# A retention and gated-MLP kernel on one core: a new instruction list for its first three blocks, chunk sums moved into another batch's results, words instead of drains, and a last tile in two halves

## The chip, the core and the metric

The kernel runs on one core of a Trainium2 chip. The metric is the device time of one execution in microseconds; before the change the median of three runs was 320.49 us (320.16 to 321.43). The engines are named here as the profile names them: PE is TensorE (PEld its weight loads), DVE is VectorE, ACT is ScalarE, POOL is GpSimd, SP is SyncE, whose queue issues most transfers.

## What is computed

For 8 batches, 8 heads, 576 positions and head size 64, a retention layer, and then a two-layer network over all 4608 rows of 512 columns:

```python
scores = scale * np.matmul(q, k.transpose(0, 1, 3, 2))
Dmat = np.where(rel >= 0, gamma[:, None, None] ** rel[None, :, :], 0.0)
attn = np.matmul(scores * Dmat[None, :, :, :], v)
x = attn.transpose(0, 2, 1, 3).reshape(B * S, H * D)
h = x @ w_in
s = np.sin(alpha * h)
g = h + s * s / (alpha + 1e-09)
out = g @ w_out
```

The decay `gamma ** rel` factors into powers of the row's and of the column's position, so that inside a chunk of 128 positions only a 0/1 mask is left, and earlier chunks enter by a state of 64 by 64 numbers for each head.

## The kernel before

The output has nine blocks of 512 rows. Blocks 0 to 7 are the first 512 positions of batches 0 to 7; block 8 gathers the last 64 positions of all eight batches ("the ends"). A block has 16 units. In a unit u TensorE projects 128 of the 2048 hidden columns (`project`, four matmuls of 128x512, line 486), ScalarE takes the sine (line 494), the square is made on VectorE, ScalarE or GpSimd (lines 503 and 505), and VectorE forms `ss/alpha + h`, the "product" (line 510). The second product, `gemm2` (line 530), adds four matmuls of 128x512 a unit; four of its units finish a tile of 128 rows, which `finish` copies (line 102) and stores. In the loop the second product of block n-1 runs in the units of block n.

The attention of batch n+1 is done during block n. k, q and v are loaded as float32 (line 113), scaled and cast (line 161, v line 104), and k and q are transposed: by TensorE for batches 0 and 1 (`turn`, line 194, and `take`), by a transposing transfer for the others (`crossed`, line 184). `scores` (line 318) makes a quarter of a batch's scores, `masked` (line 329) multiplies the mask. `outer` (line 266) makes the four chunk sums, `evict` copies them to SBUF, and `chain` turns them on GpSimd into states (`more`, `to_state`, lines 293 to 301). `values` (line 356) multiplies the masked scores with v, in a first call for the rows of one half of TensorE (`same` false) and a second for the other half (`same` true); both halves write the same PSUM bank, and so the second call waits with `nc.tensor.drain()` until the first is out of TensorE. `add_states` (line 374) adds the states' part, `keep` copies the result to the input of `project`.

PSUM has eight banks: two double banks "mm" for scores, sums and results, three banks "hp" for projections, one bank "op" for the second product. Under one tag the banks are handed out in turn.

Every engine runs its queue in the order in which the program names its steps. For the start and blocks 0 to 2 (from line 561 on) this order is a list written out step by step; from block 3 on it is a loop over units with steps attached (`at_unit`: after the sine of unit u; `behind`: at the end of unit u). Loads, stores and transposing transfers go out on SyncE's queue, the weights on GpSimd's (`load_w_in`, `load_w_out`, four groups each). The raw float32 buffers are six, so a load waits for an earlier cast. `wait_for_w_out(0)`, a small transfer that reads w_out's first group, stands on SyncE's queue between batch 0's loads and batch 1's. In the loop before, units 0, 4, 8 and 12 hold attention: scores; sums and scores; scores and the first values; the other values and the states.

## Time and profile before

| | |
|---|---|
| median of three runs | 320.49 us |
| the profiled execution | 320.69 us |
| its span, first to last instruction | 318.9 us |
| TensorE busy | 301.3 us (94%) |
| VectorE busy | 216.9 us (68%) |
| ScalarE busy | 174.0 us (55%) |
| GpSimd busy | 137.3 us (43%) |
| moved by DMA | 49.96 MB |

The profile is of one execution. Rows of the timeline give the start and the length in us, then engine, line, operation, and the tile written and those read; a bracket holds the idle time before it and what ended that. Rows that group instructions give their count, the busy time in us and the mean in ns. Ends of matmuls are modelled, so distances between starts are the safer measure on TensorE.

### The profile page before, as it was taken

Reading aid. Unit: us, or ns where it says so; the run is one execution under the profiler, and the core shown is the slowest. Engines: PE = TensorE matmul, PEld = TensorE weight load, DVE = VectorE, ACT = ScalarE, POOL = GpSimd, SP = SyncE. Lnnn points to the kernel's source line nnn. Section 1 sums busy time; section 2 is a strip of 40 time slices with the busy share of each in tenths; the row PEclk is TensorE's granted clock in tenths of the full one; section 3 lists DMA queues with packets and bytes.
Section 4 is the critical chain, followed back from the end, with each engine's and each line's share of the span. In section 5 each row is a group of like instructions: output and inputs, shape, how many; then the busy total and the mean of one; then the engine's idle time right before and its main releaser. Section 6 shows DMA issues by size and latency. Waiting matters only on the chain.

```text
span 318.9 us, 7711 instructions
## 1 busy us (share of the span) xinstructions
PE 301.3 (94%) x3180; PEld 143.9 (45%) x3180; DVE 216.9 (68%) x316; ACT 174.0 (55%) x269; POOL 137.3 (43%) x140
## 2 busy tenths in 40 slices
PE   7889999699799999999999999999999999999994
PEld 2554454244344444444444444444444444444442
DVE  2778877669468989687878787878746565655500
ACT  3548654498356645464547454745465565456411
POOL 0866542472866961993299329922720000000000
PEclk9999999799999999999999999999999999999999
DMA  8999999999994559996999589952352111111232
GB/s 211 266 202 209 299 242 280 218 239 232 213 248 144 84 113 251 262 171 134 245 255 184 123 240 257 155 113 67 72 82 49 35 35 33 36 33 34 57 77 66
DMA packets 103108, 49.96 MB, mean 157 GB/s; under 512 B 44944, under 2 KB 98592, under 8 KB 103072
## 3 DMA queue, kind: packets, MB, share of 16 engines
q1 hardware_dynamic: 98352, 45.12, 63.1%
q0 software_dynamic: 4224, 4.19, 8.0%
q8 instruction: 25, 0.41, 0.6%
q10 hardware_dynamic: 496, 0.15, 0.2%
q14 instruction: 11, 0.09, 0.1%
HBM read 36.85 MB, written 9.44 MB: 145 GB/s over the span
## 4 chain that ended last, share of the span: by engine, by line
PE 78%; DMA 9%; DVE 6%; ACT 2%; POOL 2%; issue 2%; ACTq 0%; POOLq 0%; DVEq 0%
PE hps L486 35%; PE ops L530 34%; DMA v<-in_v_dram 5%; DMA q<-in_q_dram 3%; PE sc L318 2%; PE o L356 2%; DVE gT L510 2%; DVE ret L329 2%; DVE ss_t L505 1%; DMA k<-in_k_dram 1%; PE kv L266 1%; ACT s_t L494 1%; PE o L374 1%; PE idle L543 1%; ACT ss_t L503 1%
## 5 line engine op out<-in xcount | busy, mean ns | idle before, releaser
L494 ACT ACTIVATE s_t<-hps,alpha_t 128x512 f16<-128x512 f32 x144 | 97.9, 685 | 97.1 <-PE hps L486 96.7
L530 PE MATMUL ops<-w_out,gT 128*128 128x512 f16 x580 | 144.0, 378 | 0.9 <-ACT osb L102 0.5
L510 DVE SCALAR_TENSOR_TENSOR gT<-ss_t,inva,hps 128x512 f16<-128x512 f16 x144 | 106.1, 746 | 49.4 <-ACT ss_t L503 42.1
L486 PE MATMUL hps<-xT,w_in 128*128 128x512 f16 (+1 forms) x520 | 129.3, 380 | 3.6 <-DVE xT L104 2.1
L486 PEld LDWEIGHTS <-w_in 128*128 128x128 f16 x584 | 56.8, 98 | 71.2 <-issue 5.9
L530 PEld LDWEIGHTS <-gT 128*128 128x128 f16 x580 | 54.3, 98 | 64.5 <-DVE gT L510 0.9
L505 DVE TENSOR_TENSOR ss_t<-s_t 128x512 f16<-128x512 f16 x88 | 54.0, 614 | 17.3 <-ACT s_t L494 17.2
L329 DVE TENSOR_TENSOR ret<-sc,mask 128x1024 f16<-128x1024 f32 x32 | 38.6, 1218 | 1.7 <-PE sc L318 1.6
L293 POOL TENSOR_TENSOR s<-kvs,cn 128x256 f16<-128x256 f32 x20 | 13.4, 670 | 49.4 <-ACT kvs L102 47.1
L161 POOL TENSOR_TENSOR k<-k,cn 128x1024 f16<-128x1024 f32 (+1 forms) x13 | 24.8, 1911 | 17.3 <-DMA k<-in_k_dram 17.3
L102 ACT COPY osb<-ops 128x512 f32<-128x512 f32 (+1 forms) x36 | 20.5, 573 | 16.8 <-PE ops L530 14.2
L503 ACT ACTIVATE ss_t<-s_t 128x512 f16<-128x512 f16 x45 | 28.3, 631 | 0.6
L161 POOL TENSOR_TENSOR q<-q,cn 128x1024 f16<-128x1024 f32 (+1 forms) x15 | 27.3, 1822 | 1.1 <-DMA q<-in_q_dram 1.0
L102 ACT CAST xT<-o 128x1024 f16<-128x1024 f32 (+1 forms) x16 | 13.6, 881 | 13.0 <-PE o L374 12.8
L505 POOL TENSOR_TENSOR ss_t<-s_t 128x512 f16<-128x512 f16 x11 | 11.3, 1039 | 13.4 <-ACT s_t L494 12.7
L486 PE MATMUL hps<-xS,w_in 128*128 128x512 f16 x64 | 16.4, 379 | 0.0
L104 POOL CAST v<-v 128x1024 f16<-128x1024 f32 (+1 forms) x12 | 13.0, 1084 | 6.5 <-DMA v<-in_v_dram 6.5
L301 POOL TENSOR_TENSOR kvs<-s,kvs 128x256 f32<-128x256 f32 x19 | 15.1, 792 | 1.5
L356 PE MATMUL o<-ret,v 64*64 64x128 f16 x512 | 13.0, 220 | 1.8 <-issue 0.6
L300 POOL TENSOR_TENSOR s<-kvs,cn 128x256 f32<-128x256 f32 x19 | 12.1, 635 | 2.8 <-ACT kvs L102 2.7
L318 PE MATMUL sc<-qT,kT 64*64 64x128 f16 x512 | 12.1, 220 | 0.7 <-DVE qT L104 0.4
L356 PEld LDWEIGHTS <-v 64*64 64x64 f16 x512 | 8.8, 106 | 7.9 <-issue 7.8
(52 smaller groups left out, 126.7 us busy)
## 6 DMA issues: line engine op xcount, KB each, us to landing
out_dram<-osb SPq DMA_DIRECT2D x70, 128.0 KB, 2.4
k<-in_k_dram SPq DMA_DIRECT2D x16, 512.0 KB, 6.7
q<-in_q_dram SPq DMA_DIRECT2D x16, 512.0 KB, 6.4
v<-in_v_dram SPq DMA_DIRECT2D x16, 512.0 KB, 7.1
w_in<-in_moe_w_in_dram POOLq DMA_DIRECT2D x4, 512.0 KB, 8.1
w_out<-in_moe_w_out_dram POOLq DMA_DIRECT2D x4, 512.0 KB, 10.0
ks<-in_k_dram SPq DMA_DIRECT2D x8, 128.0 KB, 5.8
qs<-in_q_dram SPq DMA_DIRECT2D x8, 128.0 KB, 3.8
```

The lines of the kernel that those rows point to most:

```text
L102: eng.copy(d_, s_)
L161: eng.tensor_tensor(dst[:, a0:a1].rearrange("p a r t d -> p t (a r) d"), t_.rearrange("p (t a) x -> p t a x", t=2)[:, :, a0:a1].rearrange( ...
L301: nc.gpsimd.tensor_tensor(self.kvs[:, c], s32, self.kvs[:, c], ADD)
L318: matmul(sc[halves(g), t, c : c + 128], kT[halves(t), 2 * a + r, halves(g)], qT[halves(t), 2 * a : 2 * a + 2, halves(g)], start=(z == 0 an ...
L329: nc.vector.tensor_tensor(ret.rearrange("p t (z x) -> p (t z) x", z=2), sc.rearrange("p t (z x) -> p (t z) x", z=2), mask[:, 0:256].unsque ...
L356: matmul(o[t][halves(e), c : c + 128], v16[halves(g), 4 * t + 2 * x + e, r, :], self.ret[p, x][halves(g), t, m : m + 128], start=(not same ...
L486: matmul(hps_of[n, fc][0][:, cols], w_in16[:, a, fc * P : (fc + 1) * P], xs[n][:, a, cols], start=(a == 0 and part != 1), stop=(a == KT - ...
L494: nc.scalar.activation(s_t, hps, mybir.ActivationFunctionType.Sin, bias=0.0, scale=alpha_t[:, fc : fc + 1],)
L503: nc.scalar.activation(ss_t, s_t, mybir.ActivationFunctionType.Square)
L505: eng.tensor_tensor(ss_t, s_t, s_t, MULT)
L510: nc.vector.scalar_tensor_tensor(gT[n][:, fc, :], ss_t, inva[:, fc : fc + 1], hps, MULT, ADD)
L530: matmul(ops[n, c][:, cols], gT[n][:, fk, c * P : (c + 1) * P], w_out16[:, fk, cols], start=(fk == 0 and cols.start == 0), stop=(fk == FC ...
```

## The change

Six things are altered together.

1. The list for the start and blocks 0 to 2 is written anew: the order of loads, casts, projections, units of the second product and attention, which engine casts and squares, and how many filling matmuls there are (29 instead of 31). `wait_for_w_out(0)` is gone; a `wait_for_w_out(2)` stands late in block 1. Many projections are made in two halves of 256 columns.
2. Each of the eight PSUM banks has a tag of its own (h0, h1, h2, op, m0, m1), and each step names its bank; the list uses all of them for projections.
3. In the loop, for n from 3 to 5, the chunk sums of batch n+2 are made in unit 12, among the results of batch n+1, into the bank of the second product and one projection bank. Scores go to units 3 and 8 (block 3 keeps 0, 4 and 8). The second product's units 12 and 13 both run behind projection 13. Loads and casts move some units, and squares of units 4, 5, 6, 8 and 9 go to ScalarE in blocks with attention.
4. In the loop the drain between the two calls of `values` is replaced: an empty instruction on GpSimd or SyncE waits for the last matmul of the first call, and the first matmul of the second call waits for it.
5. The ends of batches 0 to 3 and 4 to 7 each get one double bank and are done together, scores in unit 1, values and states in unit 8.
6. The last tile is made as two halves of 256 columns in two banks; the second half's store is issued by ScalarE.

Between the first projection and batch 1's last masked scores VectorE's queue now holds 16 products, 6 squares, 4 masked scores, four half casts of k and q, and five smaller copies and scalings; TensorE's holds 16 projections, 9 units of the second product, 4 sets of eight transposes, 64 score matmuls and 64 of chunk sums. From the second masked score of batch 2 to the end of the list VectorE's holds 7 masked scores, 18 products and 5 squares besides copies and casts, TensorE's 18 projections' worth and 14 units of the second product besides attention.

On SyncE, at the start, behind the first loads of batch 0. The names are tiles of k, q and v of batch 0, then of batch 1; before:

```order
5 L113 DMA v_96<-in_v_dram 128x8x128
6 L113 DMA v_98<-in_v_dram 128x8x128
7 L558 DMA gate<-w_out_72 128x64
8 L113 DMA k_462<-in_k_dram 128x8x128
9 L113 DMA q_464<-in_q_dram 128x8x128
```

and now:

```order
5 L114 DMA v_191<-in_v_dram 128x8x128
6 L114 DMA v_245<-in_v_dram 128x8x128
7 L114 DMA q_378<-in_q_dram 128x8x128
8 L114 DMA k_464<-in_k_dram 128x8x128
9 L114 DMA k_537<-in_k_dram 128x8x128
```

The small transfer that read w_out is gone from between the two batches.

On GpSimd at the same place, casts (q, k, v), states (s, kvs) and the issue of weights; before:

```order
7 L161 TENSOR_TENSOR k_165<-k_92,cn 128x2x4x64
8 L92 DMA w_in_71<-in_moe_w_in_dram 128x4x512
9 L161 TENSOR_TENSOR q_200<-q_94,cn 128x2x8x64
10 L92 DMA w_in_71<-in_moe_w_in_dram 128x4x512 x2
11 L300 TENSOR_TENSOR s_270<-kvs,cn 128x256
12 L301 TENSOR_TENSOR kvs<-s_270,kvs 128x256
13 L293 TENSOR_TENSOR s_273<-kvs,cn 128x256 x2
14 L95 DMA w_out_72<-in_moe_w_out_dram 128x4x512
15 L92 DMA w_in_71<-in_moe_w_in_dram 128x4x512
```

and now:

```order
12 L93 DMA w_in_71<-in_moe_w_in_dram 128x4x512
13 L105 CAST v_247<-v_245 128x1024
14 L316 TENSOR_TENSOR s_303<-kvs,cn 128x256
15 L317 TENSOR_TENSOR kvs<-s_303,kvs 128x256
16 L309 TENSOR_TENSOR s_365<-kvs,cn 128x256
17 L316 TENSOR_TENSOR s_369<-kvs,cn 128x256
18 L317 TENSOR_TENSOR kvs<-s_369,kvs 128x256
19 L309 TENSOR_TENSOR s_365<-kvs,cn 128x256
20 L93 DMA w_in_71<-in_moe_w_in_dram 128x4x512
21 L162 TENSOR_TENSOR k_534<-k_464,cn 128x2x4x64
22 L93 DMA w_in_71<-in_moe_w_in_dram 128x4x512
23 L96 DMA w_out_72<-in_moe_w_out_dram 128x4x512
```

The third group of w_in now stands behind the states of batch 0, and the fourth, with the first of w_out, behind a half cast of batch 1's k.

The list is not shown further; two of its lines stand for it in the diff below.

```diff
-        wait_for_w_out(0)
-        load(1, "k", 0)
+        load_w_in(2)
+        load(1, "q", 0)
...
+    def order(later, earlier):
+        tc.add_manual_dep(
+            later.ins,
+            earlier.ins.name,
+            mybir.DependencyInfo(mybir.DependencyClass.Sync, mybir.DependencyReason.DATA),
+            reason="rows of the two halves take turns at a bank",
+        )
+
+    def told(last, eng):
+        mark = eng.nop()
+        order(mark, last)
+        return mark
...
+        def evict_bank(self, g, eng):
+            copy(
+                eng,
+                self.kvs.rearrange("p (x g) a d -> p g x (a d)", g=2)[:, g],
+                self.banks[g].rearrange("p (x y) -> p x y", x=2),
+            )
...
+            if not same and relay is not None:
+                self.mark[p] = told(made[-1], relay)
+            elif p in self.mark:
+                order(made[0], self.mark[p])
...
+    def finish(n, c, eng=None, cols=slice(0, 512), issue=None):
...
+            (issue or nc.sync).dma_start(rows_of(n, c)[r, :, cols], osb[halves(r), cols])
...
+                if n == 3:
+                    at_unit(0, lambda: A.scores(0, 0, next(m)), lambda: A.scores(0, 1, next(m)))
...
+                    at_unit(4, lambda: A.outer((0, 1), next(m)), lambda: A.scores(1, 0, next(m)), lambda: A.evict((0, 1)))
...
+                else:
+                    at_unit(3, lambda: A.scores(0, 0, next(m)), lambda: A.scores(0, 1, next(m)))
...
+                    at_unit(8, lambda: A.scores(1, 0, next(m)), lambda: A.scores(1, 1, next(m)))
...
+                at_unit(12, lambda: A.values(0, False, next(m), relay=G_), lambda: A.values(1, False, next(m), relay=S_ if n < 6 else G_))
+                if n < 6:
+                    at_unit(12, lambda: at[n + 2].outer((0, 1), "op", next(h)))
+                at_unit(12, lambda: A.values(0, True), lambda: A.add_states(0), lambda: A.values(1, True), lambda: A.add_states(1))
...
+                    at_unit(12, lambda: at[n + 2].evict_bank(0, A_))
+                at_unit(12, lambda: A.keep(0, A_))
...
+                    at_unit(12, lambda: at[n + 2].evict_bank(1, A_))
+                    behind(12, lambda: at[n + 2].chain((0, 1, 2, 3)))
+                behind(13, lambda: A.keep(1, A_))
...
+                if n < 6:
+                    at_unit(3 + i, lambda nm=nm, p=p: cast(n + 2, nm, int(p), G_))
...
+                at_unit(8, lambda: E[0].values(False, next(m)), lambda: E[1].values(False, next(m)))
+                at_unit(8, lambda: E[0].values(True), lambda: E[1].values(True))
+                at_unit(8, E[0].add_states, E[1].add_states)
...
-        for u in range(15):
-            gemm2(NBLK - 1, u, "hp")
-            if u % 4 == 3:
-                finish(NBLK - 1, u // 4)
-        for cols in (slice(0, 256), slice(256, 512)):
-            gemm2(NBLK - 1, 15, "hp", cols)
-            finish(NBLK - 1, 3, cols=cols)
+        for c in range(3):
+            tag = next(h)
+            for u in range(4 * c, 4 * c + 4):
+                gemm2(NBLK - 1, u, tag)
+            finish(NBLK - 1, c)
+        for cols, issue in ((slice(0, 256), nc.sync), (slice(256, 512), nc.scalar)):
+            tag = next(h)
+            for u in range(12, 16):
+                gemm2(NBLK - 1, u, tag, cols)
+            finish(NBLK - 1, 3, cols=cols, issue=issue)
```

More of the change, by code (lines that the diff above doesn't have):

```diff
@@ L1 @@
 from contextlib import ExitStack
+from itertools import cycle
 import numpy as np
@@ L335, in masked, with values @@
             self.ret[p, y] = ret
-        def values(self, p, same, spare=False):
+        def values(self, p, same, *tags, relay=None):
             if same:
@@ L608 @@
[L608 to L622 removed]
+        cast(0, "q", 1, V)
+        load_w_in(0)
+        turn(0, "k", 1, "h1")
@@ new lines @@
+        take(0, "k", 1, A_)
+        at[0].scores(0, 1, "m0")
+        keep_busy(4, "h2")
+        load(0, "v", 0)
+        at[0].masked(0, 1)
+        turn(0, "q", 1, "h2")
+        take(0, "q", 1, V)
+        cast(0, "v", 0, G_)
+        at[0].outer((0,), "op", "h0")
+        load_w_in(1)
+        at[0].take_sum(0, A_)
+        load(0, "v", 1)
+        cast(0, "v", 1, G_)
+        at[0].scores(1, 0, "m1")
+        at[0].outer((1,), "op", "h1")
+        at[0].masked(1, 0)
+        at[0].take_sum(1, A_)
@@ new lines @@
+        product(0, 13)
+        at[1].masked(0, 0)
+        take(1, "q", 1, A_)
+        cast(1, "v", 0, G_)
+        at[1].outer((0,), "m1")
+        at[1].take_sum(0, A_)
+        at[1].take_sum(1, A_)
+        at[1].to_state(0, V)
+        load_w_out(3)
+        gemm2(0, 5, "h0")
+        at[1].scores(0, 1, "m1")
+        at[1].masked(0, 1)
+        at[1].scores(1, 0, "m0")
+        gemm2(0, 13, "op")
+        gemm2(0, 14, "op")
+        gemm2(0, 6, "h0")
+        cast(1, "v", 1, V, (0,))
+        at[1].masked(1, 0)
@@ L839 @@
+        sine(1, 4)
+        project(1, 11, "h1")
+        sine(1, 11)
+        square(1, 4, V)
+        product(1, 4)
+        finish(0, 2, V)
+        project(1, 8, "op", 0)
+        project(1, 8, "op", 1)
+        at[2].scores(0, 0, "m1")
+        at[2].masked(0, 0)
         sine(1, 8)
-        square(1, 8, V)
+        square(1, 8, A_)
+        square(1, 11, A_)
         product(1, 8)
-        cast(3, "k", 1, G_)
-        crossed(3, 0, "q")
-        load(4, "v", 1)
-        load(4, "k", 0)
-        at[2].scores(0, 0)
@@ new lines @@
+        square(2, 2, A_)
+        gemm2(1, 9, "h2")
+        at[3].scores(0, 0, "m1")
+        sine(2, 1)
+        at[3].outer((0, 1), "m0")
+        square(2, 3, V)
+        project(2, 7, "h1")
+        product(2, 3)
+        product(2, 2)
+        sine(2, 5)
+        square(2, 5, G_)
+        square(2, 1, V)
+        product(2, 1)
+        at[3].masked(0, 0)
+        at[3].evict((0, 1), A_)
+        at[3].more(1)
+        at[3].more(2)
+        product(2, 5)
+        cast(4, "q", 0, G_, (1,))
```

924 lines of the change are left out of this document (447 added, 477 removed).

## The prediction

> **What bounds the kernel now.** I read the stages first: a table of windows from the first projection on, cut at the end of block 0's projections, at the late start of block 1's, inside the list and at the start of block 3. Columns are the stretch, its length, the busy time of TensorE, of its weight loads, of VectorE, ScalarE and GpSimd, the granted clock, the DMA share and GB/s.
>
> ```profile
> 19.89:31.30 11.41, 11.41 (x61) 5.97 (x61) 8.75 (x18) 8.85 (x14) 6.10 (x7) 1.00 1.25 208
> 31.30:59.17 27.87, 23.46 (x326) 12.18 (x325) 22.34 (x36) 13.51 (x22) 13.16 (x11) 1.00 1.14 272
> 59.17:88.00 28.83, 25.87 (x303) 11.41 (x303) 19.21 (x27) 19.70 (x32) 16.08 (x16) 0.94 1.01 221
> 88.00:115.52 27.52, 26.89 (x321) 12.42 (x319) 22.30 (x29) 17.33 (x27) 21.66 (x22) 1.00 0.71 149
> 115.52:147.14 31.62, 31.52 (x344) 15.15 (x345) 25.78 (x34) 17.24 (x26) 20.85 (x21) 1.00 0.96 205
> ```
>
> TensorE is the bound. From 115.52 us on (the loop) it idles 0.1 us in a block of 31.6, so there the time is the work itself. The written-out list for blocks 0 to 2 is another matter: TensorE idles 4.41 us between 31.30 and 59.17, 2.96 up to 88.00 and 0.63 up to 115.52, 8.0 us in all. The timeline shows the longest of these waits, and two more windows show what it drags behind it.
>
> ```profile
> 59.17 7.46 PE L486 MATMUL hps<-xT,w_in 128*128 128x512 f16 x26 [2.12 <-DVE xT L104]
> 56.00:60.00 4.00, 1.58 (x6) 0.53 (x5) 2.56 (x2) 0.41 (x2) 3.42 (x3) 0.93 1.16 225
> 60.00:64.00 4.00, 4.00 (x13) 1.52 (x12) 2.78 (x5) 2.63 (x4) 0.00 (x0) 0.64 0.92 210
> ```
>
> After 2.12 us without a matmul the granted clock (third column from the end) is 0.93 in one window and 0.64 in the next: 4 x 0.07 + 4 x 0.36 = 1.7 us of matmul time lost. So 8.0 + 1.7 = 9.7 us is all that a better order of the list can win back after the first projection; the number of projections and of matmuls of the second product in it stays.
>
> The wait stands behind a chain of transfers. The first row below is from the timeline of SyncE: behind batch 0's last load stands a small transfer that waits for w_out, and so the first load of batch 1 goes out at 26.16. The windows show what the two kinds do to each other: weights alone move 207 GB/s, loads alone 289, and with both in flight 190. Then come the queue table for 42 to 46 us (q0 carries weights, q1 the loads) and, from the page, the size of one group of w_in.
>
> ```profile
> 26.16 0.53 SPq L113 DMA_DIRECT2D k<-in_k_dram  x1
> 22.00:26.00 4.00, 4.00 (x21) 1.81 (x19) 2.96 (x6) 3.82 (x7) 1.30 (x2) 1.00 1.24 207
> 36.00:40.00 4.00, 3.29 (x28) 1.84 (x26) 3.96 (x5) 2.04 (x5) 3.74 (x3) 1.00 1.11 289
> 42.00:46.00 4.00, 3.41 (x88) 2.22 (x90) 2.84 (x4) 2.10 (x4) 1.11 (x2) 1.00 1.09 190
> q0 software_dynamic: 493, 0.50, 82.6%
> q1 hardware_dynamic: 519, 0.26, 26.7%
> ```
>
> ```profile
> w_in<-in_moe_w_in_dram POOLq DMA_DIRECT2D x4, 512.0 KB, 8.1
> ```
>
> **The change part by part: the list.** Without the gate, batch 1's first loads go out as soon as batch 0's buffers are cast, some 15 us earlier than 26.16 by my estimate, so its data no longer ends last. What is late next? Between the first projection and batch 1's last masked scores, the new queues hold what the section on the change counts, and these groups, one of VectorE's fullest windows and three rows of TensorE's timeline give the durations.
>
> ```profile
> L510 DVE SCALAR_TENSOR_TENSOR gT<-ss_t,inva,hps 128x512 f16<-128x512 f16 x144 | 106.1, 746 | 49.4 <-ACT ss_t L503 42.1 <-POOL ss_t L505 3.9
> L505 DVE TENSOR_TENSOR ss_t<-s_t 128x512 f16<-128x512 f16 x88 | 54.0, 614 | 17.3 <-ACT s_t L494 17.2
> L329 DVE TENSOR_TENSOR ret<-sc,mask 128x1024 f16<-128x1024 f32 x32 | 38.6, 1218 | 1.7 <-PE sc L318 1.6
> L161 DVE TENSOR_TENSOR k<-k,cn 128x512 f16<-128x512 f32 x2 | 1.7, 851 | 0.3 <-DMA k<-in_k_dram 0.3
> L194 PE MATMUL tr<-ident,k 128*128 128x128 f16 x32 | 2.5, 219 | 1.1 <-DVE gT L510 0.7 <-DVE k L161 0.4
> 70.00:80.00 10.00, 9.26 (x161) 4.27 (x150) 9.19 (x12) 8.75 (x14) 4.30 (x4) 1.00 0.96 247
> 19.89 7.95 PE L486 MATMUL hps<-xT,w_in 128*128 128x256 f16 x44 [0.16 <-ACT xT L102]
> 296.68 1.03 PE L486 MATMUL hps<-xS,w_in 128*128 128x512 f16 x4
> ...
> 298.41 1.03 PE L486 MATMUL hps<-xS,w_in 128*128 128x512 f16 x4
> ```
>
> VectorE: 16 products x 0.746 = 11.9, 6 squares x 0.614 = 3.7, 4 masked x 1.218 = 4.9, 4 half casts of q and k x 0.85 = 3.4, and five smaller copies and scalings, at half such a cast each about 2.3: 26.2 us. TensorE: a unit is four matmuls, and two units lie between 296.68 and 298.41, 0.865 each; 25 units are 21.6, 64 scores and 64 chunk sums 1.8 (rows of the loop, below), 32 transposes 2.5: 25.9. The two are level, and a queue that hands work to and fro between three engines is never full: in the window from 70 to 80 us VectorE is busy 9.19 of 10. I take that, 92%: 26.2 / 0.92 = 28.5, so TensorE waits 2.6 us there. In the last stretch of the list VectorE has 7 masked, 18 products and 5 squares (8.5 + 13.4 + 3.1) and some 6 us of copies and casts, 31 us, against 33.4 us on TensorE; at 92% that is 33.7, a wait of 0.3. Waits kept: about 2.9 us in place of 9.7.
>
> The stretch before the first projection: the same six loads end it, but the four masked scores now stand behind the cast of q and one another on VectorE, and GpSimd casts both halves of v before it makes the states. Bounds: 19.89 stays (the nearest row, since the same loads and the same number of steps lie there), or 1.5 us later. I take 0.5, and 1.5 for the range. The many half-width projections cost nearly nothing: the 44 matmuls from 19.89, 16 of them half, take 7.95 us, and 28 x 0.216 + 16 x 0.108 is 7.8. The list gains 9.7 - 2.9 - 0.5 = 6.3 us; I allow 0.9, a choice, for casts that GpSimd now does one behind the other for batches 2 and 3 and for squares that crowd on ScalarE in block 1, and take **5.4**. Its ends are 10 (no wait left) and a loss (rival C).
>
> **The loop.** One block's attention sits in four places now. The timeline of TensorE shows three of them; the first number is the start.
>
> ```profile
> 217.88 1.03 PE L486 MATMUL hps<-xT,w_in 128*128 128x512 f16 x4
> 218.83 0.71 PE L266 MATMUL kv<-v,k 64*64 64x64 f16 x64
> 219.42 0.44 PE L318 MATMUL sc<-qT,kT 64*64 64x128 f16 x16
> 219.79 1.04 PE L530 MATMUL ops<-w_out,gT 128*128 128x512 f16 x4
> ...
> 226.81 0.42 PE L318 MATMUL sc<-qT,kT 64*64 64x128 f16 x16
> 227.05 0.39 PE L356 MATMUL o<-ret,v 64*64 64x128 f16 x16
> 227.38 1.04 PE L530 MATMUL ops<-w_out,gT 128*128 128x512 f16 x4
> 233.43 1.03 PE L486 MATMUL hps<-xT,w_in 128*128 128x512 f16 x4
> 234.39 0.93 PE L356 MATMUL o<-ret,v 64*64 64x128 f16 x32
> ...
> 235.81 1.04 PE L530 MATMUL ops<-w_out,gT 128*128 128x512 f16 x4
> ```
>
> Sixteen scores with more small matmuls behind them take 0.24 us (226.81 to 227.05), the same sixteen ahead of a wide matmul 0.37 (219.42 to 219.79): leaving a place costs 0.13, and entering it 0.1 (217.88 + 0.865 = 218.74, and the sums start at 218.83). A place costs 0.22. The last one, 72 small matmuls, takes 1.42 from 234.39 to 235.81; at 0.24 for sixteen that is 1.08, plus 0.13: the drain in it costs 0.2. The change merges places: blocks 3 to 6 have 13 instead of 16, the ends of the batches 2 instead of 4, so 5 x 0.22 = 1.1 saved, and six drains, 1.2. A word through GpSimd or SyncE takes their place; no row shows such a relay. In blocks 3 to 5 the 64 chunk sums (0.59) stand between, and cover it; in block 6 and at the two ends only 16 small matmuls (0.15 to 0.24) do. Bounds: nothing, or 0.5 each (a semaphore there and back); I take 0.3 x 3 = 0.9. Behind the waiting word on GpSimd stand the casts of the ends and the state chain, on SyncE the transposes of the next batch, all with a block to spare; ahead of it on GpSimd stand the six casts from unit 3 on, on an engine that was busy 20.85 us of block 3's 31.62. The bank of the second product, lent to the chunk sums, comes free when ScalarE has copied it (0.37 us for half a bank, in the end's rows); 56 small matmuls and one projection hide that. Sum: -1.1 - 1.2 + 0.9 = **-1.4**, between -2.4 and +0.5, the last if each word waited 1 us.
>
> **The last tile.** Timeline of the end:
>
> ```profile
> 313.77 0.37 ACT L102 COPY osb<-ops 128x256 f32<-128x256 f32 x1 [2.48 <-PE ops L530]
> 314.19 0.60 PE L530 MATMUL ops<-w_out,gT 128*128 128x256 f16 x4 [0.50 <-ACT osb L102]
> 314.87 0.37 ACT L102 COPY osb<-ops 128x256 f32<-128x256 f32 x1 [0.73 <-PE ops L530]
> ```
>
> The second half waits 0.50 us for the copy of the first since both lie in one bank; two banks remove that. Twenty-four more half-width matmuls are added in the place of twelve full ones, at (7.95 - 7.8) / 16 = 0.01 each some 0.2. The last transfer moves from SyncE to ScalarE, which issues it behind its own copy: 0, +-0.3. Together **-0.4**.
>
> The profiled execution took 320.69 us (span 318.9), 0.2 above the median of 320.49. 320.69 - 5.4 - 1.4 - 0.4 = **313.5 us**.
>
> **The rivals.** *A, the forecast:* 310.5 to 318.9. *B, dense:* no wait remains in the list, 320.69 - 10 - 1.4 - 0.4 = 308.9, and up to 310.5. For it: 0.63 us of idling in the 27.52 us before 115.52, at 22.30 us of VectorE. Against it: VectorE would have to be 98% full in the first stretch. *C, eaten:* VectorE at 81%, as in that same window, all along: 26.2 / 0.81 = 32.3 and 31 / 0.81 = 38.3, waits of 6.4 + 4.9; with 0.5 at the start that is 11.8 in place of 9.7, the list is 2.1 us worse, and loop and end repay 1.8: 321.0, no change. The loop's own words may also do nothing: that alone is 1.4 us and decides no sign.
>
> *D, slower: the weights starve.* GpSimd's queue now holds the third w_in group behind the states and the fourth, with w_out's first, behind the cast of batch 1's k, while batch 1's loads fill the same engines. The five groups that the first unit of the second product needs are 2.6 MB. When both kinds were in flight, weights moved 0.50 MB in 4 us; at that 125 GB/s, from about 14 us (an estimate: the first group is issued behind the cast of k's second half), they land at 35, just when TensorE comes to them (20.4 + 14 units x 0.865 and two sets of transposes, about 34). At 80 GB/s they land at 47, 12 us late; TensorE idles and loses the 1.7 us of clock besides: 313.5 + 13.7 = 327, and what is late by half of that makes 320. It decides the sign where the first unit of the second product starts later than about 43. For it: nothing holds the loads back now. Against it: in that window the weights had two thirds of the traffic.
>
> *E, even turns.* If the two kinds shared 190 GB/s evenly, weights would have 95, land at 41, 7 us late in pieces under 2 us: 313.5 + 7 = 320.5, no change. The Trainium skill ("DMA: Bandwidth & Descriptors", Queues, rings and completion order) says that each DMA engine takes turns between the queues packet by packet, which would make it E. The trace bears this out only in part: 0.50 against 0.26 MB.
>
> A wait of TensorE over 2 us is priced with the clock, as after 59.17, a shorter one without. The Trainium skill ("TensorE: Matmul & The Clock Gate", What's actually happening) lets the clock fall after an idle window of about 3.4 us; here 2.12 us of idling, with little work before it, was enough.
>
> **How the numbers follow.** A 0.58, B 0.18, C 0.06, E 0.05, D 0.13. Half a percent (1.6 us) is about what a measurement of this kernel can tell from no change: faster is under 318.9, slower over 322.1. A and B are faster, 0.76; C and E are the same, 0.11; D slower, 0.13. The range takes in B's sum with the loop's better bound (320.69 - 10 - 2.4 - 0.4 = 307.9) and on the other side most of the way to E: 308 to 320.
>
> **What would show it.** Right: block 3's first projection starts near 110 instead of 115.52, no wait of TensorE over 2 us after 20 us and no clock under 1.00 there, VectorE over 88% busy from 20 to 48 us; a loop block of about 31.2 us; no wait of TensorE in the last tile. Wrong: waits of TensorE for weights or for casts of GpSimd between 25 and 50 us (D), waits for products at each projection with VectorE near 80% (C), or waits for the word in units 12 of blocks 3 to 5.

## The result, and the profile after

The changed kernel took **313.03 us** (median of 4 runs, 312.75 to 313.92) against 320.53 us for the kernel before in the same comparison (4 runs, 320.16 to 321.43): a ratio of 0.9767, interval 0.9738 to 0.9795. The profiled execution took 313.16 us (span 311.4). The forecast was 313.5.

The stages again, cut at the first projection, at two points inside the list, and at the first projections of blocks 3, 4 and 8. The columns are those of the prediction's first table. The last row is of the kernel before, its blocks 4 to 7, which the prediction did not show.

```profile
21.69:50.90 29.21, 27.82 (x288) 15.43 (x284) 27.19 (x37) 18.65 (x32) 15.78 (x18) 0.96 1.19 245
50.90:81.00 30.10, 28.60 (x381) 15.73 (x384) 25.28 (x31) 20.22 (x32) 22.99 (x21) 1.00 1.06 242
81.00:110.95 29.95, 29.20 (x409) 15.51 (x398) 23.15 (x29) 18.53 (x28) 19.80 (x23) 1.00 0.76 174
110.95:142.83 31.88, 31.88 (x409) 15.64 (x408) 22.98 (x32) 22.82 (x36) 24.66 (x30) 1.00 0.96 206
142.83:265.69 122.86, 122.79 (x1289) 59.06 (x1288) 80.95 (x111) 78.79 (x126) 43.70 (x45) 1.00 0.61 132
```

```profile
147.14:272.51 125.37, 124.88 (x1354) 59.53 (x1352) 89.59 (x126) 71.01 (x110) 48.92 (x51) 1.00 0.59 128
```

What to see: block 3 starts at 110.95 in place of 115.52, 4.57 us earlier. Block 3 takes 31.88 (31.62 before), blocks 4 to 7 take 122.86 in place of 125.37: the loop is 2.25 us shorter. The first projection starts at 21.69, 1.80 later than before. TensorE idles 1.39 + 1.50 + 0.75 = 3.64 us in the list after its first projection (8.0 before).

TensorE's timeline, all the waits in the list that are over 0.15 us, from the last one ahead of the first projection:

```profile
20.07 0.31 PE L396 MATMUL o<-qT,s 64*64 64x128 f16 x8 [1.39 <-issue]
...
21.69 1.89 PE L509 MATMUL hps<-xT,w_in 128*128 128x256 f16 x8
23.75 9.04 PE L509 MATMUL hps<-xT,w_in 128*128 128x512 f16 x48 [0.17 <-DMA w_in<-in_moe_w_in_dram]
...
41.84 1.02 PE L552 MATMUL ops<-w_out,gT 128*128 128x512 f16 x4 [1.06 <-DMA w_out<-in_moe_w_out_dram]
...
66.12 1.03 PE L509 MATMUL hps<-xT,w_in 128*128 128x256 f16 x8 [0.69 <-DVE gT L533]
...
70.67 1.90 PE L509 MATMUL hps<-xT,w_in 128*128 128x512 f16 x12 [0.57 <-DVE gT L533]
...
110.09 1.89 PE L509 MATMUL hps<-xT,w_in 128*128 128x512 f16 x8 [0.55 <-DVE gT L533]
```

The 2.12 us behind batch 1's data are gone, and no wait is over 2 us. The eight half-width matmuls at 21.69 take 1.89 us, as long as eight full ones: the clock is halved there. Windows give the granted clock (third column from the end) and VectorE's share behind it:

```profile
20.00:24.00 4.00, 3.67 (x65) 2.37 (x65) 1.89 (x3) 1.99 (x4) 0.39 (x1) 0.57 1.17 267
24.00:28.00 4.00, 4.00 (x20) 1.80 (x19) 3.42 (x7) 3.06 (x6) 2.54 (x3) 1.00 1.19 228
28.00:44.00 16.00, 14.85 (x110) 9.12 (x108) 15.71 (x22) 12.97 (x22) 10.96 (x11) 1.00 1.19 247
```

Between 28 and 44 us VectorE is busy 15.71 of 16 us, and the DMA engines' mean busy share is over 1 throughout. Then the place of unit 12 of block 4, with the chunk sums (L275) between the two halves of the results (L374):

```profile
165.86 0.64 PE L374 MATMUL o<-ret,v 64*64 64x128 f16 x32
166.33 0.71 PE L275 MATMUL kv<-v,k 64*64 64x64 f16 x64
166.86 0.41 PE L374 MATMUL o<-ret,v 64*64 64x128 f16 x16
167.09 0.30 PE L396 MATMUL o<-qT,s 64*64 64x128 f16 x8
167.20 0.48 PE L374 MATMUL o<-ret,v 64*64 64x128 f16 x16
167.50 0.41 PE L396 MATMUL o<-qT,s 64*64 64x128 f16 x16
167.84 1.04 PE L509 MATMUL hps<-xT,w_in 128*128 128x512 f16 x4
```

Each row starts where the one before leaves off (64 chunk sums 0.53, sixteen values 0.23): nothing waits for a word. The end, from TensorE's and ScalarE's timelines:

```profile
292.46 14.88 PE L552 MATMUL ops<-w_out,gT 128*128 128x512 f16 x84
```

```profile
307.42 0.37 ACT L103 COPY osb<-ops 128x256 f32<-128x256 f32 x1 [1.37 <-PE ops L552]
```

No wait is left in the last tile. The first row holds the last unit of block 7's second product and all of block 8's; from its start to the last copy it is 307.42 - 292.46 = 14.96 us, before 314.87 - 299.27 = 15.60. From the start of that copy to the end of the span it is 3.98 us, before 4.03; the spans are given to 0.1, so that is no difference.

### The profile page after: what moved, and what is told of

Its sections match the earlier page's. It is cut to its first block, busy times and chain, and to the rows that moved or that the text cites. A ratio compares the mean times of both kernels' runs of the same rounds, so it can differ in the third digit from the quotient of the medians.

```text
span 311.4 us, 7830 instructions
## 1 busy us (share of the span) xinstructions
PE 298.4 (96%) x3238; PEld 150.7 (48%) x3238; DVE 207.3 (67%) x283; ACT 183.3 (59%) x292; POOL 140.4 (45%) x151
## 4 chain that ended last, share of the span: by engine, by line
PE 82%; DMA 6%; DVE 4%; ACT 3%; issue 2%; SPq 1%; POOL 1%; ACTq 0%; DVEq 0%
PE ops L552 38%; PE hps L509 36%; DMA w_in<-in_moe_w_in_dram 3%; PE o L374 3%; PE sc L334 2%; DMA v<-in_v_dram 2%; DVE gT L533 2%; ACT s_t L517 2%; PE kv L275 1%; SPq L114 1%; DVE ss_t L528 1%; DVE q L162 1%; PE o L396 1%; ACT ss_t L526 1%; POOL ss_t L528 0%
## 5 line engine op out<-in xcount | busy, mean ns | idle before, releaser
L552 PE MATMUL ops<-w_out,gT 128*128 128x512 f16 (+1 forms) x592 | 143.5, 374 | 1.2 <-DMA w_out<-in_moe_w_out_dram 1.1
L509 PEld LDWEIGHTS <-w_in 128*128 128x128 f16 x632 | 61.4, 98 | 66.1 <-issue 3.2
L528 DVE TENSOR_TENSOR ss_t<-s_t 128x512 f16<-128x512 f16 x67 | 40.7, 607 | 21.6 <-ACT s_t L517 21.1
L526 ACT ACTIVATE ss_t<-s_t 128x512 f16<-128x512 f16 x69 | 43.3, 630 | 1.6 <-DVE gT L533 0.5
L162 POOL TENSOR_TENSOR k<-k,cn 128x1024 f16<-128x1024 f32 (+1 forms) x17 | 29.2, 1723 | 22.4 <-DMA k<-in_k_dram 22.4
L162 POOL TENSOR_TENSOR q<-q,cn 128x512 f16<-128x512 f32 (+1 forms) x16 | 24.4, 1537 | 7.5 <-DMA q<-in_q_dram 6.1
L317 POOL TENSOR_TENSOR kvs<-s,kvs 128x256 f32<-128x256 f32 x23 | 17.2, 747 | 5.3 <-ACT kvs L103 3.8
L146 POOL TENSOR_TENSOR ks<-ks,cn 128x512 f16<-128x512 f32 x4 | 4.2, 1043 | 29.3 <-PE o L374 29.3
L316 POOL TENSOR_TENSOR s<-kvs,cn 128x256 f32<-128x256 f32 x23 | 14.1, 613 | 3.6 <-ACT kvs L103 3.3
L103 ACT COPY kvs<-kv 128x256 f32<-128x256 f32 (+2 forms) x15 | 7.9, 548 | 10.1 <-PE kv L275 8.4
L374 PE MATMUL o<-ret,v 64*64 64x128 f16 x512 | 12.3, 222 | 1.3 <-DVE ret L345 0.7
```

Source lines behind the costliest of these rows:

```text
L103: eng.copy(d_, s_)
L162: eng.tensor_tensor(dst[:, a0:a1].rearrange("p a r t d -> p t (a r) d"), t_.rearrange("p (t a) x -> p t a x", t=2)[:, :, a0:a1].rearrange( ...
L317: nc.gpsimd.tensor_tensor(self.kvs[:, c], s32, self.kvs[:, c], ADD)
L374: made.append(matmul(o[t][halves(e), c : c + 128], v16[halves(g), 4 * t + 2 * x + e, r, :], self.ret[p, x][halves(g), t, m : m + 128], sta ...
L509: matmul(hps_of[n, fc][0][:, cols], w_in16[:, a, fc * P : (fc + 1) * P], xs[n][:, a, cols], start=(a == 0 and part != 1), stop=(a == KT - ...
L526: nc.scalar.activation(ss_t, s_t, mybir.ActivationFunctionType.Square)
```

## The experiments

The theory after the result: the loop gains by its merged places and by the words, the list by loads that start early in a fitting order; what the list did not gain sits before 44 us. The rivals: the places or the drains give nothing by themselves; or un-gating the loads does it all; and for the rest, a cold start (waits and clock), VectorE, or the weights. Times are compared by their ratio to the kernel before; the intervals are 0.2 to 0.4% to each side, some 0.9 us.

| run | us | ratio to before (interval) |
|---|---|---|
| changed kernel | 313.03 | 0.9767 (0.9738 to 0.9795) |
| e1_gate | 321.44 | 1.0035 (1.0013 to 1.0056) |
| e2_drains | 314.36 | 0.9813 (0.9787 to 0.9840) |
| e3_places | 314.96 | 0.9830 (0.9804 to 0.9857) |
| e4_start | 313.57 | 0.9783 (0.9758 to 0.9808) |
| e5_hold | 313.52 | 0.9794 (0.9766 to 0.9822) |
| e6_vector | 314.81 | 0.9831 (0.9804 to 0.9857) |
| e7_early | 313.57 | 0.9791 (0.9764 to 0.9818) |
| e8_fill | 313.42 | 0.9789 (0.9762 to 0.9816) |
| e9_qcast | 313.42 | 0.9793 (0.9759 to 0.9827) |
| e10_casts | 313.33 | 0.9787 (0.9754 to 0.9821) |
| e11_both | 313.50 | 0.9798 (0.9761 to 0.9835) |
| e12_swap | 313.12 | 0.9775 (0.9746 to 0.9804) |

Where the list alone is at stake, the start of block 3's first scores is a finer measure: 111.90 in the changed kernel. e2 and e3, whose list is the same, have 111.28 and 111.46; so a difference there counts from about 0.6 us on.

**e1: the gate alone, taken from the kernel before.**

```diff
-        wait_for_w_out(0)
         load(1, "k", 0)
```

> The kernel before with one line gone: the small transfer that waits for w_out in front of batch 1's loads. Theory one (the late loads make the 2.12 us wait at 59.17 and the half clock behind it): the loads go out as buffers come free, some 10 us earlier; the wait at 59.17 and most of the idling from 31 to 59 us go, and the time falls by 2 to 5 us, to 315.5 to 318.5. Theory two (the order of the queues makes the waits, the loads were early enough): 320 to 321. Theory three (weights starve when loads fill the same engines): the first unit of the second product starts 3 us or more later than before, and the time is 322 or more.

Measured: 1.1 us slower than before, by the ratio. The timeline of TensorE says why (first row: the last of batch 0's results, in the kernel before; second row: the same matmuls in e1; third row: the first projection; the window is that of the prediction's table):

```profile
18.44 0.24 PE L356 MATMUL o<-ret,v 64*64 64x128 f16 x2 [0.63 <-issue]
...
19.55 0.24 PE L356 MATMUL o<-ret,v 64*64 64x128 f16 x2 [1.89 <-issue]
...
21.48 4.42 PE L486 MATMUL hps<-xT,w_in 128*128 128x256 f16 x24
27.56 4.49 PE L486 MATMUL hps<-xT,w_in 128*128 128x512 f16 x20 [1.65 <-DMA w_in<-in_moe_w_in_dram]
38.52 1.02 PE L530 MATMUL ops<-w_out,gT 128*128 128x512 f16 x4 [1.29 <-DMA w_out<-in_moe_w_out_dram]
42.24 2.75 PE L530 MATMUL ops<-w_out,gT 128*128 128x512 f16 x12 [0.70 <-DMA w_out<-in_moe_w_out_dram]
```

```profile
19.89:31.30 11.41, 9.68 (x92) 5.51 (x85) 5.96 (x13) 6.80 (x11) 3.16 (x5) 0.86 1.20 216
```

The wait of 2.12 us at 59.17 is gone, as theory one has it, but the weights now come late (3.6 us of waits that were not there) and the clock falls to 0.86 in the first stretch. The first unit of the second product starts at 31.89 in place of 27.84, the sign that theory three named, though the time stays just under its 322. The first projection, too, starts 1.59 us later than before (21.48 against 19.89), with nothing changed ahead of it but the loads; most of that is the wait in the first two rows, of which e4 and e5 tell more. So the late loads did make the long wait, and early loads do starve the weights where the order of the queue is the old one: no theory holds alone. Taking out the gate needs the new order; whether the new order would have gained with the gate left in was not tried.

**e2: drains again.**

```diff
-                at_unit(12, lambda: A.values(0, False, next(m), relay=G_), lambda: A.values(1, False, next(m), relay=S_ if n < 6 else G_))
+                at_unit(12, lambda: A.values(0, False, next(m)), lambda: A.values(1, False, next(m)))
...
-                self.mark = told(made[-1], G_)
+                open_turns.append(self)
```

> The changed kernel with drains of TensorE again in place of GpSimd's and SyncE's words, one for each of blocks 3 to 6 and one for the ends, five in all. Theory one (a drain costs 0.2 us here, a word nothing): places of unit 12 take 0.2 longer each, 1.0 us in all, 314.0 in place of 313.0. Theory two (the gain of the loop is the merged places, drains in merged places cost nothing): 313.0, and the place of unit 12 of block 4 takes 1.98 us as now.

Measured: the place of unit 12 of block 4 takes 168.17 - 165.70 = 2.47 us, against 167.84 - 165.86 = 1.98 with the words.

```profile
165.70 0.64 PE L374 MATMUL o<-ret,v 64*64 64x128 f16 x32
166.17 0.73 PE L275 MATMUL kv<-v,k 64*64 64x64 f16 x64
167.26 0.42 PE L374 MATMUL o<-ret,v 64*64 64x128 f16 x16 [0.37 <-issue]
...
168.17 1.04 PE L509 MATMUL hps<-xT,w_in 128*128 128x512 f16 x4
```

The other places, by the same reading: blocks 3 and 5 the same 0.5, block 6, where no chunk sums stand ahead of the drain, 1.65 against 1.45, the ends 1.56 against 1.52. That is 1.7 in all. The whole takes 1.3 us more than the changed kernel by the medians, its span 1.1 more; the list ended 0.62 earlier in this execution, so what lies behind it took 1.7 more. A drain costs 0.2 behind the results of block 6, 0.5 behind 64 chunk sums and hardly anything in the ends, and the words cost nothing that shows. Theory one, with a larger price in three places.

**e3: seven more places.**

```diff
-                    at_unit(3, lambda: A.scores(0, 0, next(m)), lambda: A.scores(0, 1, next(m)))
+                    at_unit(3, lambda: A.scores(0, 0, next(m)))
+                    at_unit(4, lambda: A.scores(0, 1, next(m)))
```

and in the same way for the pairs at units 8 and 9, and at units 0 and 1 of block 3.

> The changed kernel with pairs of scores pulled apart again: the second of each pair goes one unit later, seven more places among wide matmuls (one in block 3, two each in blocks 4 to 6). Theory one (entering and leaving a place costs 0.22 us): 7 x 0.22 = 1.5 us, 314.6; blocks 4 and 5 take 0.44 longer each. Theory two (places cost nothing, the loop gained by its drains): 313.0 and blocks of 31.06 us as now.

Measured: from block 4's first scores to block 5's,

```profile
148.74 0.42 PE L334 MATMUL sc<-qT,kT 64*64 64x128 f16 x16
...
180.24 0.42 PE L334 MATMUL sc<-qT,kT 64*64 64x128 f16 x16
```

it is 31.50 us, against 31.06 in the changed kernel (148.97 to 180.03): 0.44 for two places, 0.22 each, to the hundredth what the prediction took. By the medians the kernel is 1.9 us slower than the changed one, its span 1.1 longer; 1.5 were expected. The list ended 0.44 earlier here, so what lies behind it took 1.5 longer. Theory one.

**e4 and e8: the start.** In both, three idle matmuls more stand in each of the waits for v and for the masked scores, and the first unit that needs w_in's second group comes two units later; e4 has 21 opening matmuls, e8 all 24.

```diff
-        keep_busy(1, "h2")
+        keep_busy(4, "h2")
...
-        project(0, 6, "h1")
...
         project(0, 2, "m0")
...
         project(0, 3, "h2")
...
+        project(0, 6, "h1")
```

> The changed kernel with three changes ahead of and at the first projections: 21 opening matmuls in place of 24; three idle matmuls more in each of the two waits for v and for the masked scores; and the fifth projection group's first unit, which needs the second group of w_in, two units later. Theory one (waits of 0.76, 0.69 and 1.39 us within 5 us halve the clock from 21 to 24 us, and the second w_in group lands only at 23.7): with the waits filled and no unit waiting for weights the clock stays at 1.00, the 1.7 us lost to it come back, and the first transposes start up to 0.5 us earlier: 311 to 311.8. Theory two (VectorE has the first stretch in its hands anyway, so TensorE only waits later): 312.5 to 313.5. Theory three (the 1.39 us wait ahead of the states is for GpSimd's states): it stays as it is and ends with to_state on GpSimd; if it is a matter of code loading it moves to another instruction when matmuls are added ahead of it.

> The changed kernel with its 24 opening matmuls, three idle matmuls more in each of the two waits for v and for the masked scores, and the first unit that needs w_in's second group two units later. Theory one (the clock fell because of the waits of 0.76, 0.69 and 1.39 us; the run with 21 opening matmuls only made a new wait of 1.54 us further ahead): the clock stays at 1.00 from 16 to 24 us, and the 1.7 us come back less what the fill costs, some 0.3: 311.5 to 312.2. Theory two (weights and VectorE take up whatever the clock gives): 313.0 to 313.5.

Measured: no gain in either. Of e4, the wait that has no releaser, the waits for weights, and the start of block 3:

```profile
21.04 0.25 PE L374 MATMUL o<-ret,v 64*64 64x128 f16 x3 [1.02 <-issue]
...
30.11 3.46 PE L509 MATMUL hps<-xT,w_in 128*128 128x512 f16 x16 [0.47 <-DMA w_in<-in_moe_w_in_dram]
...
42.61 1.02 PE L552 MATMUL ops<-w_out,gT 128*128 128x512 f16 x4 [1.26 <-DMA w_out<-in_moe_w_out_dram]
...
110.16 1.89 PE L509 MATMUL hps<-xT,w_in 128*128 128x512 f16 x8 [0.56 <-DVE gT L533]
```

In e4 the granted clock is 1.00 from 20 to 44 us, the first projection comes at 22.50, TensorE waits for weights twice, and block 3 starts where it did. What the half clock costs is better seen in e2: with the same list as the changed kernel its clock stayed at 1.00 from 20 to 28 us, and TensorE waited 1.19 us for w_in's second group and 1.15 for w_out's first in place of 0.17 and nothing:

```profile
21.50 1.12 PE L509 MATMUL hps<-xT,w_in 128*128 128x256 f16 x8 [0.15 <-ACT xT L103]
23.80 8.83 PE L509 MATMUL hps<-xT,w_in 128*128 128x512 f16 x48 [1.19 <-DMA w_in<-in_moe_w_in_dram]
...
38.27 1.04 PE L552 MATMUL ops<-w_out,gT 128*128 128x512 f16 x4 [1.15 <-DMA w_out<-in_moe_w_out_dram]
```

Block 3's scores came 0.62 earlier. In e3, with the same list once more, the clock fell to 0.57 from 20 to 24 us as in the changed kernel, and the scores came only 0.18 behind e2's. So in these three executions the half clock cost between 0.2 and 0.6 us, since the weights set the pace then. In e8 the clock still falls (0.72 from 20 to 24 us, 0.85 in the next four) and block 3's first scores come at 113.01, 1.1 later. The wait of 1.39 us is not for the states (theory three of e4 asked that). In e4 three more matmuls stand ahead of it than in the changed kernel, and it stops TensorE three matmuls earlier in the program; in e8 it is six and six:

```profile
20.34 0.30 PE L374 MATMUL o<-ret,v 64*64 64x128 f16 x6 [1.77 <-issue]
```

In the kernel before, too, TensorE stops at this same place of its program, the 223rd matmul from the start (0.63 us), and so does every run here. Each time a packet of the queue of kind "instruction" goes ahead of the end of the wait: from 16 to 17 us before, from 17 to 18 after, from 18 to 19 in e4 and e8; TensorE goes on 1.3 to 1.5 us after the packet's end in all of them. So it is TensorE's code that comes late.

**e5: batch 1's later loads held,** to see whether the loads make the code late.

```diff
+        nc.sync.dma_start(gate, w_in16[:, 0, 0:64])
         load(1, "k", 1)
```

> The changed kernel with batch 1's later loads held: in SyncE's queue a small transfer that waits for the first group of w_in stands ahead of the load of k's second part. Theory one (the un-gated loads fill the DMA engines from 12 to 20 us, so that TensorE's next packet of code and the first groups of w_in come late): the packet starts near 17 in place of 17.84, the wait of 1.39 us ahead of the states shrinks to under 0.7, w_in's second group lands by 22 in place of 23.70, the clock stays at 1.00 from 20 to 24 us, and block 3's first projection comes 1.5 to 2.5 us earlier: 310.5 to 311.5. Theory two (the code load does not care about the loads): the wait stays at 1.4 and the time at 313, or up to 315 if batch 1's k and q then land after 32 us, where they are wanted.

Measured: time and wait are those of theory two. The wait for code is 1.25 us and its packet goes where it did; TensorE, whose clock was 0.57 from 20 to 24 us again, does not wait for w_in's second group, and waits 1.41 us in place of 1.06 for w_out's second one.

```profile
20.06 0.43 PE L396 MATMUL o<-qT,s 64*64 64x128 f16 x8 [1.25 <-issue]
```

But the run does not put theory one to the test: what it held was not moving yet. From 14 to 20 us the queue of the loads carried 0.66 MB in this run as in the changed kernel, and the two differ from 22 us on. The pair that does put it to the test is e1 and the kernel before, which differ in the gate alone. From 14 to 20 us the queue of the loads carried nothing before and 0.64 MB in e1, beside the weights; the code's packet started at 16.16 before and at 17.22 in e1, and TensorE stood 0.63 us for it before and 1.89 in e1. So early loads do make the code late, as far as one execution of each can tell.

**e6: four more operations for VectorE.**

```diff
+        nc.vector.tensor_tensor(more, zero, zero, MULT)
```

behind the products of units 3, 4, 8 and 10 of block 0.

> The changed kernel with four more VectorE multiplications of 128x512 f16 (what they give is used by nothing) between the first projections and batch 1's first scores: 4 x 0.61 = 2.5 us of VectorE time at the price of the trace before, 1.7 at the 0.42 us of the shorter squares after. Theory one (VectorE and TensorE are level in this stretch, as the prediction had it): block 3's first projection comes 1.5 to 2.5 us later, 314.5 to 315.5. Theory two (TensorE alone sets the stretch, VectorE's share of 93% is slack that it takes up): 0 to 0.5 us later, 313.0 to 313.5.

Measured: 1.8 us slower than the changed kernel by the medians, and block 3's first scores at 113.09, 1.2 later. Two of the four took 0.41, two 0.62 and 0.89 us (2.3 in all). TensorE now waits for VectorE where it did not wait:

```profile
33.19 1.46 PE L509 MATMUL hps<-xT,w_in 128*128 128x512 f16 x8 [1.68 <-DVE gT L533]
```

So VectorE has about 1 us of slack in this stretch and no more: nearer to theory one.

**e7: w_out's second group issued earlier.**

```diff
-        cast(1, "k", 1, G_)
         load_w_out(1)
+        cast(1, "k", 1, G_)
```

> The changed kernel with the second w_out group issued one GpSimd cast earlier. Theory one (the wait of 1.06 us at 41.84 is for this group alone): the group goes out 1.0 to 2.5 us earlier, the wait goes, block 3's first projection comes up to 1.0 us earlier: 312.0 to 312.8. Theory two (VectorE holds the stretch, which is full to 96% there): TensorE waits for VectorE at the next step instead: 313.0.

Measured: no gain. GpSimd's timeline has the issue at 30.25 (32.33 in the changed kernel), TensorE's the end of the wait:

```profile
30.25 0.80 POOL L96 DMA_DIRECT2D w_out<-in_moe_w_out_dram  x1
```

```profile
41.91 1.02 PE L552 MATMUL ops<-w_out,gT 128*128 128x512 f16 x4 [0.82 <-DMA w_out<-in_moe_w_out_dram]
```

Issued 2.08 us earlier, it lands no earlier (41.84 there). The rate of the transfers decides, not the moment of issue: a third thing that neither theory had named.

**e9, e10, e11: VectorE relieved of casts.** In e9 one half cast of batch 1's q goes to GpSimd, in e10 one of its k too, and e11 is e10 with e7's edit.

```diff
-        cast(1, "q", 1, V, (1,))
+        cast(1, "q", 1, G_, (1,))
```

> The changed kernel with one half cast of batch 1's q moved from VectorE to GpSimd, behind the other half. On VectorE this cast took 2.65 us at 39.33, where the same cast took 0.69 with GpSimd idle; GpSimd's three casts ran from 39.39 to 42.7 just then. Theory one (VectorE, 98% busy from 28 to 44 us, sets the first stretch, and it stands still while GpSimd works): VectorE gets 2.65 us back, GpSimd takes 1.05 more, of which it has some; block 3's first projection comes 0.8 to 1.5 us earlier, 311.5 to 312.3. Theory two (w_out's wait of 1.06 us at 41.84 covers it): 312.8 to 313.3. Theory three (GpSimd then delivers q and v too late, 44 us and on): 313.5 to 314.5.

> As the run before, and the half cast of batch 1's k that VectorE did at 29.46 (1.16 us) moved to GpSimd too, ahead of its square of unit 5, in a gap of 2.4 us. Theory one (VectorE sets the stretch): up to 1.2 us more than the run before, 310.5 to 311.8. Theory two (another wait takes its place: w_out's second group at 41.8): the same as the run before.

> As the run before, with w_out's second group issued one GpSimd cast earlier besides. That alone gave nothing (313.57 against 313.03), with VectorE full at 28 to 44 us. Theory one (VectorE first, weights next): with VectorE relieved the wait for w_out is the next to end last, and the earlier issue is worth 0.5 to 1.0 us: 310 to 311.3. Theory two (the weights' transfers take as much longer as they start earlier): the same as the run before.

Measured: no gain in any. In the changed kernel VectorE (first two rows) needs 2.65 us for a cast that took it 0.69 at the start, and GpSimd (last two) is casting for most of that while:

```profile
5.12 0.69 DVE L162 TENSOR_TENSOR q<-q,cn 128x512 f16<-128x512 f32 x1 [3.95 <-DMA q<-in_q_dram]
...
39.33 2.65 DVE L162 TENSOR_TENSOR q<-q,cn 128x512 f16<-128x512 f32 x1
```

```profile
39.39 1.05 POOL L162 TENSOR_TENSOR q<-q,cn 128x512 f16<-128x512 f32 x1
40.38 1.04 POOL L105 CAST v<-v 128x1024 f16<-128x1024 f32 x1
```

In e9 the next operation of VectorE takes the blow, a square of 0.42 us, which ends only when GpSimd's three casts are over (42.57 + 1.03 = 43.60):

```profile
41.28 2.61 DVE L528 TENSOR_TENSOR ss_t<-s_t 128x512 f16<-128x512 f16 x1 [0.24 <-ACT s_t L517]
```

```profile
40.58 2.05 POOL L162 TENSOR_TENSOR q<-q,cn 128x512 f16<-128x512 f32 x2
42.57 1.03 POOL L105 CAST v<-v 128x1024 f16<-128x1024 f32 x1
```

Work given from VectorE to GpSimd so comes back as standing still. The Trainium skill ("SBUF — State Buffer", SBUF: two separate sides) says that the two engines share a pair of ports which one of them holds for a whole instruction while the other is blocked; these rows agree, 2.65 against 0.69 and 2.61 against 0.42, with the addition that here VectorE came in only at the end of several casts. That is no rule: in the changed kernel a VectorE square of 2.05 us ended at 65.22, while GpSimd cast on until 66.12.

**e12: later use of the weights, and v's cast on ScalarE.**

```diff
-        gemm2(0, 1, "h1")
+        gemm2(0, 4, "h0")
...
+        cast(1, "v", 0, A_)
...
-        gemm2(0, 4, "h0")
+        gemm2(0, 1, "h1")
...
-        cast(1, "v", 0, G_)
```

> The changed kernel with two edits where the transfers of the weights and GpSimd's casts hold the list. The second product's unit that needs w_out's second group, for which TensorE waits 1.06 us until 41.8 (the group landed between 41.8 and 43.6 whether it went out at 30.25 or at 33.98), changes places with one that needs the first group, behind the transposes of q. And the cast of batch 1's v goes from GpSimd, where it keeps VectorE standing at 40.38 to 41.42, to ScalarE, which is idle then for 1.66 us. Theory one (up to 42 us the transfers set the pace, so asking later for the weights frees TensorE where issuing them earlier did not): the wait of 1.06 us shrinks to 0.4 or less, the long VectorE cast of 2.65 to about 1.7, and block 3's first projection comes 0.6 to 1.2 us earlier, 311.8 to 312.6. Theory two (VectorE's work alone sets the stretch, and it frees 1.0): 312.0 to 312.6 with a wait for VectorE in place of the one for w_out. Theory three (what is gained by 50 us is lost again at the three waits of 0.5 to 0.7 for VectorE in block 1): 313.0.

Measured: 313.12, block 3's first scores at 111.76: theory three, with another place for the loss than it named. VectorE's cast takes 1.58 in place of 2.65 and the square behind it 0.42; the wait at 41.84 is down to 0.43, and ScalarE's copy of the transposed q ends it, no longer the weights. But in this execution the clock stayed at 1.00, and TensorE waits earlier for the two groups ahead of that one:

```profile
23.92 8.83 PE L509 MATMUL hps<-xT,w_in 128*128 128x512 f16 x48 [1.06 <-DMA w_in<-in_moe_w_in_dram]
38.40 1.04 PE L552 MATMUL ops<-w_out,gT 128*128 128x512 f16 x4 [1.17 <-DMA w_out<-in_moe_w_out_dram]
42.04 1.02 PE L552 MATMUL ops<-w_out,gT 128*128 128x512 f16 x4 [0.43 <-ACT qT L103]
```

No version was measurably faster than the changed kernel.

## Why the prediction was right, point by point

The time (313.5 against 313.03), the sign and the mechanism held. The three terms of the sum were all off in size: forecast -5.4, -1.4 and -0.4, measured -4.57 (start of block 3), -2.25 (loop) and -0.69 (end), -7.5 in the span. The list gained 0.8 less and loop and end 1.1 more than forecast; that the total came within 0.5 us is in part luck.

**TensorE bounds the loop, and the list idles.** This was right. In the loop TensorE is busy 31.88 of 31.88 us and 122.79 of 122.86.

**The list's term, -5.4: several parts were off.** *The start,* taken as 0.5, was 1.8 late. The step that failed is that 19.89 was the nearest row "since the same loads and the same number of steps lie there": batch 1's loads, no longer gated, now move there too. TensorE comes to the matmul at which it stands for its code 0.87 us later than before (with waits of 0.76 and 0.69 us for v's cast and the masked scores on the way), stands there 0.76 longer (1.39 against 0.63), and takes 0.17 more from there to the first projection. e1 against the kernel before shows what the gate does to this: with it alone taken out, the wait for code grew by 1.26 us and the first projection came 1.59 later. How the 0.87 divides between the loads and the new order is open. *The waits kept,* forecast at 2.9, were 3.64 of idling. What they are for was forecast wrongly: VectorE was to cause them in the first stretch. It is as full there as forecast (27.19 of 29.21, 93%) and e6 shows it close to the bound, but the wait that remains, 1.06 us, is for w_out. (Five copies at half of 0.85 us are 2.1, not 2.3, so by its own rows that wait came to 2.4 and not 2.6.) The stretch from batch 1's last masked scores to the second of batch 2 had no term at all; in it lie the waits of 0.69 and 0.57 us for products (66.12 and 70.67). *The clock* fell once more: 1.00 was forecast, 0.57 came from 20 to 24 us. Against e2's rows at full clock the matmuls behind the first projection took 1.0 us longer (1.89 against 1.12 and 9.04 against 8.83); e2 and e3 show that 0.2 to 0.6 of it counts, since weights bind there. *Not foreseen, on the other side:* the list, too, merges places. Counted in TensorE's timelines, small matmuls stand among wide ones at 18 places between the first projection and block 3 before and at 12 after; at e3's 0.22 that is 1.3 us. As an account of TensorE's time: 9.7 + 1.3 - 3.6 - 1.0 - 1.8 = 4.6, against 4.57 measured. The 1.3 is worked out from the loop's price and was not measured in the list.

**Rival D, the weights.** It was right that this would not decide the sign: the first unit of the second product starts at 37.56, far from 43. Its five groups landed at 37.52 in place of 35, and in the changed kernel TensorE came at 37.56, so "just when TensorE comes to them" held, with the groups 2.5 and TensorE 3.5 us later than forecast; in e12 and in e2, where the clock did not fall, w_in's second group and w_out's first held it 1.06 to 1.19 each. What had no price was the next group: the second of w_out landed between 41.7 and 43.6 us in all versions of the changed kernel, issued between 30.25 (e7) and 33.98 (e8), and it held TensorE for 0.8 to 1.4 us in most. e1 shows the rival at work in the old order: there it ate the whole gain of the early loads.

**The allowance of 0.9 for GpSimd's casts.** It was a choice for batches 2 and 3, and the trace shows something of it there: the waits of 0.69 and 0.57 us for products stand behind VectorE squares that took 2.05 us (at 63.17) and 1.15 us (at 68.62) in place of 0.42, while GpSimd cast. What they cost in the end was not tried, nor was the cause of the 0.55 at block 3. The stand of 2.2 us in e9's rows is another, on batch 1's casts, which the allowance did not name.

**The loop, -1.4.** The places at 0.22 are shown by e3 to the hundredth. The drains at 0.2 each are shown by e2 for one place without chunk sums, block 6; in the ends it was 0.04. The failed step is the price of the words, 0.9: no row waits for one, and e2 gives no sign of a cost. Without it the forecast is -1.1 - 1.2 = -2.3, measured -2.25; that the two agree so closely is more than six drains at 0.2 can claim, if those of the ends cost less.

**The last tile, -0.4.** The mechanism was right: the wait of 0.50 is gone. A slip stands in the sum: 0.50 won and 0.2 paid make 0.3, not 0.4. Measured are 15.60 - 14.96 = 0.64: the 24 extra half-width matmuls cost nothing that shows, and some 0.14 more was won, which no row explains. The last store from ScalarE's queue makes no difference that shows, as was taken.

**The rivals.** B wanted VectorE at 98%: it is that from 28 to 44 us, and still TensorE waited for weights. C took a low share of VectorE for a sign of waits. In the two later stages of the list the share is 25.28 of 30.10 and 23.15 of 29.95, 84% and 77%, and TensorE idles 1.50 and 0.75 us there, so that step of C fails. E's even turns would have put the weights 7 us late in pieces; TensorE's waits for them add up to 1.2 us in the changed kernel and to 2.6 in e2 at full clock. The prediction misread its own queue table here: 493 packets of weights and 519 of loads are even turns, packet by packet, just as the rule that it cites has them. The weights had twice the bytes because their packets were twice as large (0.50 MB in 493 against 0.26 MB in 519), so even turns never meant an even share of the 190 GB/s.

**The signs it named.** Block 3's first projection came at 110.95 (near 110), VectorE was busy 89% from 20 to 48 us (over 88%), block 4 took 31.06 us from scores to scores (about 31.2), and no wait was over 2 us or in the last tile. One sign failed: the clock was not 1.00 throughout.

## What to carry to other kernels

A wait at the end of a chain of transfers can be removed by taking out the gate that holds the chain, but that alone need not win time: removed in the old order of the queues, the gate left the kernel 0.35% slower (e1). When several single reliefs give nothing, as e4 and e7 to e12 did here, look for resources that are level: up to 44 us the transfers, VectorE and TensorE seem to have been each within about 1 us of being the bound, so each relief ended at the next one. And look in the trace whether an edit did what it was made for before reading anything from its time: e5 left the stretch that it was to relieve as it was. Small matmuls are best kept in few places, and a word through an idle queue in place of a drain costs nothing where other small matmuls stand between.

## What the runs showed of the hardware

- A drain of TensorE behind the 64 chunk sums cost 0.5 us, behind values of 64x128 0.2, in the ends 0.04 (e2).
- TensorE stood for 0.63 to 1.89 us at the 223rd matmul, whatever stood there, until 1.3 to 1.5 us after a packet of code (every run). With batch 1's loads moving at that time the packet started 1.06 us later and the wait was 1.26 longer (e1 against the kernel before).
- Two queues with work took turns packet by packet: 493 and 519 packets from 42 to 46 us (before), 0.50 and 0.26 MB.
- VectorE's casts and squares stood still while GpSimd cast: 0.42 us became 2.61 (e9).
- The granted clock fell to 0.50 from 21 to 24 us in the changed kernel behind waits of 0.76, 0.69 and 1.39 us. In e12 it stayed at 1.00 behind waits of 0.73, 0.67 and 1.65 at the same places. What decides it stays open.
